# An attention and MLP kernel on one core: an earlier front with fp32 beacon transposes, and batch 1's k and q loaded ahead of the last quarter of the first weight matrix

## The chip, the cores and the metric

One core of one Trainium2 chip. The metric is the device time of one execution in microseconds (us). Quoted times are medians of fast executions; most executions of one kernel lie within 1 us of its median, single ones up to 4 us above it. An execution more than 1.5% above the fastest of its kernel is called slow here and left out of every ratio. The span that a trace shows is about 1.7 us shorter than the time.

## The reference

Attention for 8 batches of 8 heads over 576 tokens, with 16 "beacon" keys and values ahead of each sequence, then an MLP with a squared relu over all 4608 tokens. In short:

```python
# q, k, v: [8, 8, 576, 64]; beacon_k, beacon_v: [8, 8, 16, 64]
# w_in: [512, 2048]; w_out: [2048, 512]
k_all = np.concatenate([beacon_k, k], axis=2)
v_all = np.concatenate([beacon_v, v], axis=2)
scores = np.matmul(q, k_all.transpose(0, 1, 3, 2)) / np.sqrt(64)
scores = np.where(causal, -1e9, scores)
a = softmax(scores)
x = np.matmul(a, v_all).transpose(0, 2, 1, 3).reshape(4608, 512)
g = np.maximum(x @ w_in, 0.0) ** 2
out = g @ w_out
```

## The kernel before

The program is a list of operations with modelled durations. A scheduler of the kernel's own, run while the program is built, sorts them into one fixed order for each engine; on the chip each engine runs its list in that order and waits by semaphores only for data and buffers. Where the model sees TensorE idle in the first 22 us it inserts a filler, a product of zeros, meant to have the array at full clock early.

```python
    def emit_fill(bank, cols):
        nc.tensor.matmul(ps[bank][:, 0:cols], g[1][:, 0, 0:128], g[1][:, 0, 0:cols], start=True, stop=True)
...
    # Order.run: nothing is ready for engine e at the modelled time now
    if e == "PE" and 0.3 < now < self.FILL_UNTIL and self.pools["ps"]:
        cols = 128 if now < 7.0 else 256
        ...
```

Transfers of the first two batches and of the weights go through GpSimd's queue one behind the other (`t` tables, `p1k` pair 1's k, `v0` the first part of v, `w0` a quarter of w_in); then comes batch 1's k and q, then batch 1's v.

```python
    SOFT = "t0 p1k p1q t1 p2k p2q v0 v1 p3k p3q v2 v3 v4 w0 w1 w2 w3".split()
    ...
    strided[1, 0, 0, "k"].behind[:] = chain[-1:]
    v_loads[1][0].behind[:] = [strided[1, 0, HP - 1, "q"]]
```

A v part lands as fp32 and GpSimd casts it to bf16. VectorE applies the causal masks, does relus together with ScalarE, and squares. TensorE's first layer writes into one of four PSUM banks, which comes free when the relu has read it.

```python
        def emit_cast(e):                      # GpSimd, for batch 1's v
            st = stg[ld.held[2]]
            if x == "v":
                copy_on(e, vb[b % 2][0:rows, c, :, 0:D], st[0:rows])
        ...
        def emit_mask(e):                      # VectorE, two inputs in SBUF
            ...
                nc.vector.tensor_tensor(out=d, in0=d, in1=tri[:, m0:m0 + m, :][:, None].to_broadcast([128, 2, m, 128]),
                                        op=ALU.min)
        ...
        def emit_relu(e, ft=ft, lo=lo_ - t0, hi=hi_ - t0, box=box):
            h = ps[box["s1"].held[2]][:, 0:hi - lo]       # one input, in PSUM
            ...
                nc.vector.tensor_scalar(out=dst, in0=h, scalar1=0.0, scalar2=None, op0=ALU.max)
        ...
        def emit_sq(e, f=f, lo=lo_ - t0, hi=hi_ - t0):    # two inputs in SBUF
            nc.vector.tensor_tensor(out=d, in0=d, in1=d, op=ALU.mult)
```

The softmax here doesn't subtract the row's maximum and nothing guards it: scores larger than these inputs give would overflow.

Of the kernel before, what the change touches and what calls it, by code (L numbers as in the profile page):

```python
# [9 lines left out]
FP32 = mybir.dt.float32  # L10
# [36 lines left out]
class Order:  # L47
# [22 lines left out]
    def run(self):  # L70
# [16 lines left out]
        free = {e: 2.3 if e == "DVE" else 0.0 for e in engines}  # L87
        dma_free = 0.0
        lanes = {"SP": [], "POOL": [], "ACT": []}
        events = [(0.0, 0, None, None)]  # L90
# [3 lines left out]
        now = 0.0  # L94
        while events:
# [19 lines left out]
            while again:  # L115
                again = False
                for e in engines:
# [26 lines left out]
                    if best is None:  # L144
                        if e == "PE" and 0.3 < now < self.FILL_UNTIL and self.pools["ps"]:
                            cols = 128 if now < 7.0 else 256
                            free[e] = now + 0.107
                            issued.append((Op("fill", "PE", 0.107, lambda e, cols=cols, bank=self.pools["ps"][0]: self.fill(bank, cols)), e, now))
                            seq += 1
                            heapq.heappush(events, (free[e], seq, "free", None))  # L150
                        continue
# [51 lines left out]
def kernel(  # L203
# [63 lines left out]
    bkf = [sb("bkf", [Nb, H, D], FP32)] * 2  # L267
    bks = [sb(f"bks{i}", [Nb, H, D], BF16) for i in range(2)]
# [45 lines left out]
    ident_op = add("ident", "POOL", 1.3, lambda e: make_identity(nc, ident), prio=-300.0)  # L314
    tri_ops = [add(f"tri{i}", "POOL", (0.95, 0.55)[i], lambda e, i=i: emit_tri(e, i), prio=-250.0) for i in range(2)]
# [39 lines left out]
    def add_load(b, x, c, prio, behind=[], sync=[]):  # L355
# [34 lines left out]
        if x != "v":  # L390
            if b < NPE + 2:
                deps += [zero_ops[b]]
            else:
# [4 lines left out]
                            late=(5.0 if b else 1) if x == "v" else 0.0)  # L398

    def add_trans(b, x, prio):  # L400
        srcb, dst = (qb, qT) if x == "q" else (kb, kT)

        def emit(e):
            nc.sync.dma_start(
                out=dst[b % 2].rearrange("p g (c t) -> p (g c) t", c=NT),
                in_=srcb[b % 2].rearrange("p g c d -> p (g c d)"),
                transpose=True,
            )

        deps = [cast[b, x, c] for c in range(NT)]  # L410
        deps += [o for p in range(HP * (b - 2), HP * (b - 1)) for o in qk_ops[p]]
        trans[b, x] = [add(f"tr{b}{x}", "SP", 4.1, emit, prio=prio, deps=deps, dma=3.7, late=3.0)]

    def add_beacon(b, prio):
        prio = prio if b else -299.5
        ld = add(f"bkl{b}", "SP", 0.45, lambda e: [nc.sync.dma_start(
            out=bkf[b % 2], in_=beacon_k[b].transpose([1, 0, 2]))], prio=prio, dma=0.1,
                 deps=[cast[b - 1, "bk"]] if b else [])
        bk = add(f"bkc{b}", "DVE", 0.4, lambda e: nc.vector.tensor_copy(bks[b % 2], bkf[b % 2]), prio=prio,
                 deps=[ld])  # L420
        cast[b, "bk"] = bk
        if b:
            bk.need.extend(norm_ops[HP - 1, 0])
        box = {}

        def emit_tp(e):
            pp = ps[box["t"].held[2]].bitcast(BF16)
            for pr in range(HP):
                nc.tensor.transpose(pp[:, pr * Nb:(pr + 1) * Nb], bks[b % 2][:, 2 * pr:2 * pr + 2, :], ident[0:Nb, 0:Nb])

        busy = [o for pr in range(HP) for o in qk_ops[HP * (b - 2) + pr]] if b >= 2 else []
        box["t"] = add(f"tpb{b}", "PE", 0.25, emit_tp, prio=prio - 100.0, deps=[bk, ident_op], take=("ps", "tp"))

        def emit_ev(e):
            pp = ps[box["t"].held[2]].bitcast(BF16)
            copy_on(e, kT[b % 2][:, :, 0:Nb], pp[:, 0:HP * Nb].rearrange("p (g n) -> p g n", g=HP))

        bk_ev[b] = add(f"ekb{b}", "DVE", 0.2, emit_ev, prio=-200.0, deps=[box["t"]] + busy, give=box["t"])

    bk_ev = {}  # L440

# [17 lines left out]
    def add_strided(b, prio):  # L459
# [7 lines left out]
        for part, (t0, np_, ns, prs) in enumerate(parts_of[b]):  # L467
            n_tok = np_ * ns
            own = b == 0 and part < 2
            for pr in prs:  # L470
                groups = ["kq"] if 2 * n_tok <= 1024 else ["k", "q"]
                for n, xs in enumerate(groups):
# [20 lines left out]
                    for i, x in enumerate(xs):  # L493
# [6 lines left out]
                        if b == 0:  # L500
                            engs = ("DVE",)
                        else:
                            engs = ("DVE",) if x == "k" else ("DVE", "ACT")
                        ev = add(f"e{x}{b}.{part}.{pr}", engs,
                                 {"DVE": 0.12 + n_tok / 960.0, "ACT": 0.2 + n_tok / 1200.0}, emit_ev,
                                 prio=(-200.0 if x == "k" else -199.0) + 0.01 * part, deps=[tp])
# [5 lines left out]
    def add_first_loads():  # L512
        first = []
        at = 0
        for part in range(2):
            t0, np_, ns, _ = parts_of[0][part]
            for n, (x, t) in enumerate((("k", k), ("q", q))):
# [3 lines left out]
                def emit(e, t=t, n=n, raw=raw, t0=t0, np_=np_, ns=ns):  # L521
# [3 lines left out]
                o = add(f"fld{x}{part}", ("SP", "ACT")[n], (0.45, 0.55)[n], emit, prio=-300.0 + part,  # L525
                        dma={"k": (0.3, 0.75), "q": (0.55, 0.65)}[x][part])
                first.append(o)

                def emit_cast(e, x=x, raw=raw, part=part):
                    copy_on(e, paired_buf(x, part).rearrange("p s (u d) -> p u s d", u=2), raw)  # L530

                strided[0, part, 0, x] = add(f"fc{x}{part}", ("DVE", "ACT")[n],
                                             ((0.33, 0.75)[part], (0.42, 0.52)[part])[n], emit_cast,
                                             prio=-210.0 + part, deps=[o], late=0.3)
# [63 lines left out]
    RANK = [(0, 0), (0, 1), (1, 0), (2, 0), (1, 1), (3, 0), (2, 1), (3, 1)]  # L598
# [37 lines left out]
    PLAN = ((2,2,3,3,3),(2,2,3,3,3),(2,3,3,3,2),(2,3,3,3,2),(2,3,3,3,2),(2,3,3,3,2),(2,3,3,3,2))  # L636
# [339 lines left out]
    SOFT = "t0 p1k p1q t1 p2k p2q v0 v1 p3k p3q v2 v3 v4 w0 w1 w2 w3".split()  # L976
# [60 lines left out]
    v_loads[1][0].behind[:] = [strided[1, 0, HP - 1, "q"]]  # L1037
# [33 lines left out]
```

## Time and profile before

| before | |
|---|---|
| time, median of 4 runs | 337.98 us (337.48 to 338.21) |
| span of the trace | 335.8 us |
| TensorE busy | 327.9 us, 98% |
| TensorE's waits for another engine | 1.1 us at the start, 0.7 us for batch 1's first k |
| full clock from | 4.2 us |

TensorE sets the time. How the lines are read is told with the prediction, which shows the front and the wait. These are VectorE, GpSimd and TensorE in the timeline of the kernel before (start, length, engine, line, operation, shapes, count, idle before with its releaser):

```profile
41.70 0.94 DVE L712 TENSOR_TENSOR pt<-pt,tri 128x512 bf16<-128x512 bf16 x2
...
39.29 0.62 POOL L327 CAST vb<-stg 128x512 bf16<-128x512 f32 x1 [0.22 <-DMA stg<-in_v_dram]
40.78 0.70 POOL L327 CAST vb<-stg 80x512 bf16<-80x512 f32 x1
...
41.61 2.38 PE L901 MATMUL ps<-xT,w_in 128*128 128x272 bf16 x20
```

Two masks take 0.94 us together. They begin at 41.70, 0.22 us after GpSimd's last cast of batch 1's v has ended (41.48); the matmuls of the first layer have no wait.

### The profile page before, as it was taken

How to read it: one execution, taken by the hardware profiler on the slowest of the kernel's cores; microseconds unless marked ns; L12 is line 12 of the kernel's file. 1: busy time of each engine (PE TensorE's matmuls, PEld its weight loads, DVE VectorE, ACT ScalarE, POOL GpSimd, SP SyncE). 2: the span in 40 equal slices, each digit the busy share in tenths (PEclk: the TensorE clock that was granted, in tenths of full speed). 3: DMA queues.
4: the chain of work that ended last, by engine and by line, in shares of the span. 5: the costliest groups of instructions: out<-in, count | busy, mean ns of one | idle time of the engine just before them, and what ended most of it. 6: DMA issues, size and time to landing. Idle time of an engine off the chain costs nothing.

```text
span 335.8 us, 7815 instructions
## 1 busy us (share of the span) xinstructions
PE 327.9 (98%) x3156; PEld 188.1 (56%) x3197; DVE 170.8 (51%) x389; ACT 191.1 (57%) x291; POOL 92.7 (28%) x145
## 2 busy tenths in 40 slices
PE   8999999999999999999999999999999999999996
PEld 7586765544654655555459845554555544444444
DVE  5786885238645983477147733573457302301400
ACT  4976865377638827565466655666457216515621
POOL 9874803316404614041134132423000000000000
PEclk9999999999999999999999999999999999999999
DMA  8999989999999999899799997999210221011003
GB/s 153 193 207 220 208 143 208 222 240 211 193 215 232 197 184 184 185 232 176 146 239 235 174 186 183 249 186 167 76 62 2 46 90 62 0 64 62 1 2 124
DMA packets 143955, 51.74 MB, mean 154 GB/s; under 512 B 130702, under 2 KB 138798, under 8 KB 143918
## 3 DMA queue, kind: packets, MB, share of 16 engines
q1 hardware_dynamic: 135375, 42.19, 61.6%
q0 software_dynamic: 7904, 8.69, 14.9%
q8 instruction: 25, 0.41, 0.5%
q10 hardware_dynamic: 639, 0.36, 0.4%
q14 instruction: 12, 0.10, 0.1%
HBM read 37.22 MB, written 9.44 MB: 139 GB/s over the span
## 4 chain that ended last, share of the span: by engine, by line
PE 89%; DMA 5%; POOL 4%; issue 1%; ACT 0%; POOLq 0%
PE ps L901 36%; PE ps L939 36%; PE ps L738 8%; PE strip L620 5%; DMA qk_area<-in_k_dram 3%; PE ps L620 2%; DMA stg<-in_v_dram 2%; POOL qk_area L449 1%; PE ps L851 1%; PE ps L484 1%; POOL stg L371 1%; PE ps L805 1%; POOL w_in L830 0%; POOL vb L327 0%; POOL tri L311 0%
## 5 line engine op out<-in xcount | busy, mean ns | idle before, releaser
L901 PE MATMUL ps<-xT,w_in 128*128 128x512 bf16 (+3 forms) x689 | 133.3, 340 | 0.9 <-issue 0.2
L939 PE MATMUL ps<-w_out,g 128*128 128x512 bf16 x534 | 126.3, 379 | 2.0 <-issue 0.8
L901 PEld LDWEIGHTS <-w_in 128*128 128x128 bf16 x704 | 65.4, 98 | 51.4 <-issue 0.7
L917 ACT ACTIVATE g<-ps 128x512 bf16<-128x512 f32 (+2 forms) x118 | 66.3, 562 | 43.1 <-PE ps L901 42.5
L629 ACT ACTIVATE pt<-strip 128x1024 bf16<-128x1024 f32 (+3 forms) x86 | 81.3, 1002 | 12.1 <-PE strip L620 11.9
L926 DVE TENSOR_TENSOR g<-g 128x1024 bf16<-128x1024 bf16 (+2 forms) x80 | 52.7, 666 | 63.3 <-ACT g L917 62.2
L939 PEld LDWEIGHTS <-g 128*128 128x128 bf16 x560 | 51.5, 98 | 56.8 <-issue 1.7
L327 POOL CAST qk_area<-stg 128x512 bf16<-128x512 f32 (+2 forms) x60 | 40.3, 677 | 61.5 <-DMA stg<-in_k_dram 35.1
L325 ACT COPY osb<-ps 128x512 f32<-128x512 f32 (+2 forms) x29 | 16.4, 569 | 65.2 <-PE ps L939 60.5
L327 POOL CAST vb<-stg 128x512 bf16<-128x512 f32 (+1 forms) x40 | 26.4, 671 | 70.7 <-DMA stg<-in_v_dram 67.3
L738 PEld LDWEIGHTS <-pt 128*128 128x128 bf16 (+1 forms) x960 | 36.2, 97 | 10.1 <-DVE pt L712 0.2
L738 PE MATMUL ps<-vb,pt 128*128 128x65 bf16 (+1 forms) x960 | 39.0, 194 | 0.0
L712 DVE TENSOR_TENSOR pt<-pt,tri 128x512 bf16<-128x512 bf16 x64 | 29.6, 472 | 12.0 <-ACT pt L629 6.7
L757 DVE TENSOR_TENSOR xn<-ps,rcp 128x320 bf16<-128x320 f32 (+2 forms) x64 | 31.5, 492 | 2.3
L919 DVE TENSOR_SCALAR g<-ps 128x512 bf16<-128x512 f32 (+2 forms) x42 | 24.7, 606 | 13.8 <-PE ps L901 13.2
L671 ACT ACTIVATE pt<-ps 128x512 bf16<-128x512 f32 x42 | 22.8, 597 | 13.7 <-PE ps L620 11.1
L620 PEld LDWEIGHTS <-kT 64*128 64x128 bf16 x596 | 19.8, 94 | 16.0 <-issue 14.2
L755 DVE RECIPROCAL rcp<-ps 128x5 f32<-128x5 f32 (+2 forms) x64 | 12.2, 191 | 30.0 <-PE ps L738 29.1
L620 PE MATMUL strip<-qT,kT 64*128 64x208 bf16 (+13 forms) x474 | 27.0, 239 | 0.0
L327 DVE COPY osb<-ps 128x512 f32<-128x512 f32 (+1 forms) x9 | 5.8, 647 | 33.4 <-PE ps L939 17.4
L295 PE MATMUL ps<-g 128*128 128x128 bf16 (+1 forms) x83 | 10.1, 274 | 1.1 <-DVE warm L302 1.1
L371 POOL DMA_DIRECT2D stg<-in_v_dram x10 | 8.5, 859 | 5.7 <-DMA w_in<-in_moe_w_in_dram 4.4
(42 smaller groups left out, 98.3 us busy)
## 6 DMA issues: line engine op xcount, KB each, us to landing
out_dram<-osb SPq DMA_DIRECT2D x17, 512.0 KB, 4.1
stg<-in_q_dram SPq DMA_DIRECT2D x24, 256.0 KB, 5.1
stg<-in_k_dram SPq DMA_DIRECT2D x18, 256.0 KB, 5.1
stg<-in_v_dram SPq DMA_DIRECT2D x18, 256.0 KB, 4.5
w_in<-in_moe_w_in_dram POOLq DMA_DIRECT2D x4, 512.0 KB, 8.1
w_out<-in_moe_w_out_dram POOLq DMA_DIRECT2D x4, 512.0 KB, 11.1
stg<-in_v_dram POOLq DMA_DIRECT2D x6, 256.0 KB, 7.6
stg<-in_k_dram SPq DMA_DIRECT2D x6, 224.0 KB, 4.5
```

The source lines that it names most:

```text
L327: eng[e].tensor_copy(dst, src)
L620: nc.tensor.matmul(st[hj][:, at:at + t1 - t0], kT[b % 2][hp, pr, 128 * c:128 * c + 128], qT[b % 2][hp, pr, t0:t1], start=True, stop=True,)
L629: nc.scalar.activation(pt[:, :, at:at + width], strips[qk.slots[s]][:, :, 0:width], AF.Exp, bias=0.0, scale=scale)
L671: nc.scalar.activation(pt[:, hj, at:at + 512], ps[qk.wide[hj]], AF.Exp, bias=0.0, scale=scale)
L712: nc.vector.tensor_tensor(out=d, in0=d, in1=tri[:, m0:m0 + m, :][:, None].to_broadcast([128, 2, m, 128]), op=ALU.min)
L738: nc.tensor.matmul(a[:, at + (t - tl[0]) * (D + 1):at + (t - tl[0] + 1) * (D + 1)], P[0:rr, hj, o:o + 128], vb[b % 2][0:rr, c, 2 * pr + hj ...
L757: nc.vector.tensor_tensor(out=xn[b % 2].rearrange("p t (h d) -> p h t d", d=D)[:, h0:h0 + nh, tl[0]:tl[0] + nt], in0=a[:, :, :, 0:D], in1= ...
L901: nc.tensor.matmul(h[:, lo - spans[0][0]:hi - spans[0][0]], w_in_sb[:, mc, ft * 128:(ft + 1) * 128], xT[:, mc, lo % RING:lo % RING + hi - lo],
L917: nc.scalar.activation(dst, h, AF.Relu, bias=0.0, scale=1.0)
L919: nc.vector.tensor_scalar(out=dst, in0=h, scalar1=0.0, scalar2=None, op0=ALU.max)
L926: nc.vector.tensor_tensor(out=d, in0=d, in1=d, op=ALU.mult)
L939: nc.tensor.matmul(o, G[:, fc, ts * 128:(ts + 1) * 128], w_out_sb[:, fc, :], start=(fc == 0), stop=(fc == NFT - 1))
```

## The change

The intent: begin real work sooner (k cast and transposed without waiting for q, the beacon transposed in fp32 without a cast), load the last pair's q and k ahead of v, and take away TensorE's wait for batch 1's k by loading batch 1's k and q ahead of w_in's last quarter. The core of the diff:

```diff
-                        if e == "PE" and 0.3 < now < self.FILL_UNTIL and self.pools["ps"]:
-                            cols = 128 if now < 7.0 else 256
+                        if e == "PE" and 0.9 < now < self.FILL_UNTIL and self.pools["ps"]:
+                            cols = 128 if now < 6.0 else 256
...
+    ident32_op = add("ident32", "DVE", 0.1, lambda e: nc.vector.tensor_copy(ident32, ident[0:Nb, 0:Nb]), prio=-300.0, deps=[ident_op])
...
-                            late=(5.0 if b else 1) if x == "v" else 0.0)
+                            late=(5.0 if b > 2 else 3.0 if b else 1) if x == "v" else 0.0)
...
-        bk = add(f"bkc{b}", "DVE", 0.4, lambda e: nc.vector.tensor_copy(bks[b % 2], bkf[b % 2]), prio=prio,
-                 deps=[ld])
...
-                nc.tensor.transpose(pp[:, pr * Nb:(pr + 1) * Nb], bks[b % 2][:, 2 * pr:2 * pr + 2, :], ident[0:Nb, 0:Nb])
+                nc.tensor.transpose(ps[box["t"].held[2]][:, pr * Nb:(pr + 1) * Nb], bkf[:, 2 * pr:2 * pr + 2, :], ident32)
...
-                groups = ["kq"] if 2 * n_tok <= 1024 else ["k", "q"]
+                groups = ["kq"] if 2 * n_tok <= 1024 and not own else ["k", "q"]
...
-    PLAN = ((2,2,3,3,3),(2,2,3,3,3),(2,3,3,3,2),(2,3,3,3,2),(2,3,3,3,2),(2,3,3,3,2),(2,3,3,3,2))
+    PLAN = ((2,2,3,3,3),(2,2,2,2,2,2,1),(2,3,3,3,2),(2,3,3,3,2),(2,3,3,3,2),(2,3,3,3,2),(2,3,3,3,2))
...
-    SOFT = "t0 p1k p1q t1 p2k p2q v0 v1 p3k p3q v2 v3 v4 w0 w1 w2 w3".split()
+    SOFT = "t0 p1k p1q t1 p2k p2q p3k p3q v0 v1 v2 v3 v4 w0 w1 w2".split()
...
-    v_loads[1][0].behind[:] = [strided[1, 0, HP - 1, "q"]]
+    w_ops["in", 3].behind[:] = [strided[1, 0, HP - 1, "q"]]
+    v_loads[1][0].behind[:] = [w_ops["in", 3]]
```

Left out: modelled durations of the first loads and casts, a choice of engines for them, a rank of score phases, and names.

More of the change, by code (lines that the diff above doesn't have):

```diff
@@ L86, in run @@
                 release(op)
-        free = {e: 2.3 if e == "DVE" else 0.0 for e in engines}
+        free = {e: {"DVE": 2.3, "ACT": 0.05}.get(e, 0.0) for e in engines}
         dma_free = 0.0
         lanes = {"SP": [], "POOL": [], "ACT": []}
-        events = [(0.0, 0, None, None)]
+        events = [(0.0, 0, None, None), (0.05, 0, None, None)]
         seq = 0
@@ L265, in paired_buf @@
             "p (s e) -> p s e", s=parts_of[0][part][2])
-    bkf = [sb("bkf", [Nb, H, D], FP32)] * 2
-    bks = [sb(f"bks{i}", [Nb, H, D], BF16) for i in range(2)]
+    bkf = sb("bkf", [Nb, H, D], FP32)
+    ident32 = sb("ident32", [Nb, Nb], FP32)
     vb = [sb(f"vb{i}", [128, NT, H, D + 1], BF16) for i in range(2)]
@@ L411, in add_trans @@
         deps += [o for p in range(HP * (b - 2), HP * (b - 1)) for o in qk_ops[p]]
-        trans[b, x] = [add(f"tr{b}{x}", "SP", 4.1, emit, prio=prio, deps=deps, dma=3.7, late=3.0)]
+        trans[b, x] = [add(f"tr{b}{x}", "SP", 4.1, emit, prio=prio, deps=deps, dma=3.7, late=3.0 if b > 2 else 1.5)]
     def add_beacon(b, prio):
-        prio = prio if b else -299.5
+        prio = prio if b else -298.5
         ld = add(f"bkl{b}", "SP", 0.45, lambda e: [nc.sync.dma_start(
-            out=bkf[b % 2], in_=beacon_k[b].transpose([1, 0, 2]))], prio=prio, dma=0.1,
-                 deps=[cast[b - 1, "bk"]] if b else [])
-        bk = add(f"bkc{b}", "DVE", 0.4, lambda e: nc.vector.tensor_copy(bks[b % 2], bkf[b % 2]), prio=prio,
-                 deps=[ld])
-        cast[b, "bk"] = bk
-        if b:
-            bk.need.extend(norm_ops[HP - 1, 0])
+            out=bkf, in_=beacon_k[b].transpose([1, 0, 2]))], prio=prio, dma=0.1,
+                 deps=[bk_tp[b - 1]] if b else [])
         box = {}
         def emit_tp(e):
-            pp = ps[box["t"].held[2]].bitcast(BF16)
             for pr in range(HP):
-                nc.tensor.transpose(pp[:, pr * Nb:(pr + 1) * Nb], bks[b % 2][:, 2 * pr:2 * pr + 2, :], ident[0:Nb, 0:Nb])
+                nc.tensor.transpose(ps[box["t"].held[2]][:, pr * Nb:(pr + 1) * Nb], bkf[:, 2 * pr:2 * pr + 2, :], ident32)
         busy = [o for pr in range(HP) for o in qk_ops[HP * (b - 2) + pr]] if b >= 2 else []
-        box["t"] = add(f"tpb{b}", "PE", 0.25, emit_tp, prio=prio - 100.0, deps=[bk, ident_op], take=("ps", "tp"))
+        box["t"] = bk_tp[b] = add(f"tpb{b}", "PE", 0.25, emit_tp, prio=prio - 100.0,
+                                  deps=[ld, ident32_op] + (norm_ops[HP - 1, 0] if b else []), take=("ps", "tp"))
         def emit_ev(e):
-            pp = ps[box["t"].held[2]].bitcast(BF16)
-            copy_on(e, kT[b % 2][:, :, 0:Nb], pp[:, 0:HP * Nb].rearrange("p (g n) -> p g n", g=HP))
+            copy_on(e, kT[b % 2][:, :, 0:Nb], ps[box["t"].held[2]][:, 0:HP * Nb].rearrange("p (g n) -> p g n", g=HP))
         bk_ev[b] = add(f"ekb{b}", "DVE", 0.2, emit_ev, prio=-200.0, deps=[box["t"]] + busy, give=box["t"])
     bk_ev = {}
+    bk_tp = {}
     def add_part_load(b, part, prs, x, prio, behind, free, dma, late=0.0):
@@ L500, in add_strided @@
                         if b == 0:
-                            engs = ("DVE",)
+                            engs = ("ACT", "DVE") if own and part == 1 and x == "q" else ("DVE",)
                         else:
@@ L505, in add_strided @@
                                  {"DVE": 0.12 + n_tok / 960.0, "ACT": 0.2 + n_tok / 1200.0}, emit_ev,
-                                 prio=(-200.0 if x == "k" else -199.0) + 0.01 * part, deps=[tp])
+                                 prio=(-200.0 if x == "k" else -199.0) + 0.01 * part - (500.0 if b == 0 and part == 2 else 0.0), deps=[tp])
                         evs.append(ev)
@@ L523, in emit @@
                         out=raw, in_=t[0, 0:2, t0:t0 + np_ * ns, :].rearrange("h (p s) d -> p h s d", s=ns))]
-                o = add(f"fld{x}{part}", ("SP", "ACT")[n], (0.45, 0.55)[n], emit, prio=-300.0 + part,
-                        dma={"k": (0.3, 0.75), "q": (0.55, 0.65)}[x][part])
+                o = add(f"fld{x}{part}", ("SP", "ACT")[n], (0.6, 0.55)[n], emit, prio=-300.0 + part,
+                        dma={"k": (0.43, 0.15), "q": (0.37, 0.85)}[x][part])
                 first.append(o)
@@ L530, in emit_cast @@
                     copy_on(e, paired_buf(x, part).rearrange("p s (u d) -> p u s d", u=2), raw)
-                strided[0, part, 0, x] = add(f"fc{x}{part}", ("DVE", "ACT")[n],
-                                             ((0.33, 0.75)[part], (0.42, 0.52)[part])[n], emit_cast,
-                                             prio=-210.0 + part, deps=[o], late=0.3)
+                strided[0, part, 0, x] = add(f"fc{x}{part}", (("DVE",), ("ACT",))[n] if part == 0 or x == "q" else ("ACT", "DVE"),
+                                             {"DVE": (0.46, 0.6)[part], "ACT": (0.42, 0.52)[part]}, emit_cast,
+                                             prio=-210.0 + 20.0 * part, deps=[o], late=0.1)
             at += 2 * ns * D
@@ L597 @@
     NSPLIT = HP
-    RANK = [(0, 0), (0, 1), (1, 0), (2, 0), (1, 1), (3, 0), (2, 1), (3, 1)]
+    RANK = [(0, 0), (0, 1), (1, 0), (1, 1), (2, 0), (3, 0), (2, 1), (3, 1)]
     def phases(p):
```

## The prediction

> **What bounds the kernel now.** I read the page first, then TensorE's list of waits, then its timeline over the first 38 us, then the chain of waits and the landings of the transfers in the same stretch.
>
> The page and TensorE's list of waits, the whole kernel:
>
> ```profile
> PE 327.9 (98%) x3156; PEld 188.1 (56%) x3197; DVE 170.8 (51%) x389; ACT 191.1 (57%) x291; POOL 92.7 (28%) x145
> L295 PE MATMUL ps<-g 128*128 128x128 bf16 (+1 forms) x83 | 10.1, 274 | 1.1 <-DVE warm L302 1.1
> ...
> PE ps L295 <- DVE warm L302: 1.1, 1, 1.1
> PE ps L939 <- issue: 0.8, 5, 0.2
> PE ps L484 <- DMA qk_area<-in_k_dram: 0.7, 1, 0.7
> PE ps L901 <- issue: 0.2, 1, 0.2
> ```
>
> TensorE works 327.9 of 335.8 us. It waits for another engine just twice: 1.1 us at the start, and 0.7 us for batch 1's first k. The 0.2 us entries marked "issue" have the length of one 512-column matmul (216 ns from start to start) and lie between equal matmuls, many of them about 10.8 us apart: records missing from the trace, not waits. But 83 of TensorE's matmuls are fillers (L295, zeros into a spare bank), put into its fixed order wherever the kernel's own scheduler thought it would be idle. They always run. So "98% busy" holds some 8 us of nothing, and the time is the sum of a fixed list plus its waits.
>
> TensorE's timeline where the change bites:
>
> ```profile
> 1.12 3.40 PE L295 MATMUL ps<-g 128*128 128x128 bf16 x32 [1.12 <-DVE warm L302]
> 4.37 0.38 PE L481 MATMUL ps<-ident,qk_area 120*128 120x120 bf16 x4
> 4.68 0.25 PE L429 MATMUL ps<-ident,bks 16*128 16x16 bf16 x4
> 4.86 1.01 PE L295 MATMUL ps<-g 128*128 128x128 bf16 x15
> 5.80 0.47 PE L481 MATMUL ps<-ident,qk_area 112*128 112x112 bf16 x6
> 6.20 0.34 PE L620 MATMUL strip<-qT,kT 64*128 64x240 bf16 x4
> ...
> 10.25 0.83 PE L295 MATMUL ps<-g 128*128 128x256 bf16 x6
> 11.01 0.35 PE L620 MATMUL strip<-qT,kT 64*128 64x336 bf16 x4
> ...
> 24.49 1.39 PE L901 MATMUL ps<-xT,w_in 128*128 128x240 bf16 x12
> 25.72 0.31 PE L805 MATMUL ps<-ident,xn 128*128 128x128 bf16 x3
> 25.87 2.78 PE L901 MATMUL ps<-xT,w_in 128*128 128x240 bf16 x24
> 29.37 0.70 PE L484 MATMUL ps<-ident,qk_area 96*64 96x96 bf16 x24 [0.71 <-DMA qk_area<-in_k_dram]
> ```
>
> Columns: start, length, engine, line, tiles, count, idle before. Between 1.12 and 28.6 us TensorE never idles: in the front it arrives later than its operands, because of the fillers. At 29.37 it is early.
>
> The chain of waits over the same stretch names the loads behind that wait:
>
> ```profile
> 16.07 1.36 POOL vb L327 x2
> 17.43 1.42 POOL w_in L830 x2
> 18.84 10.48 DMA qk_area<-in_k_dram
> 29.32 0.04 issue
> 29.37 0.70 PE ps L484 x24
> ```
>
> The load takes 10.48 us because it stands in the GpSimd queue behind w_in. From the landings: w_in's quarters at 22.8, 25.3 and 28.0 us (the last issued at 18.1, 9.9 to land), then batch 1's k and q at 29.3, 30.8, 32.3 and 33.8. So a quarter costs 2.7 us of that queue, a half batch of k or q 1.5.
>
> [...]fillers of 128 columns start 107 ns apart until 4.3 us, then 56 ns. [...]six 256-column fillers, 109 ns apart, take 0.65 us, and the scores after them start 0.76 us after the first; I count about 0.09 us at each switch. [...]the first k load (120 KB) takes 2.6 us to land, so there is nothing to gain ahead of 3.4 us.[...]
>
> **The change, part by part**, read from the order in which both programs' instructions stand on each engine. I take the TensorE list from the first transpose up to batch 1's first k transposes: in the kernel before that is 4.37 to about 28.49 us, 24.12 us of work.
>
> Start. The fillers ahead of the first transpose go from 32 to 21, so they end at 1.12 + 21 x 0.107 = 3.37. k alone then needs its load (0.80 + 2.6 = 3.4) and the 0.46 us cast on VectorE: about 3.95. So TensorE starts real work at 4.0 instead of 4.37: -0.37, with 0.6 us of idle time in place of fillers. q's own cast (3.85 + 0.40) is ready for its turn.
>
> First scores. k part 1 is loaded ahead of the beacon: issued at about 1.3 instead of 1.74, so landed at 4.7. VectorE casts it to 5.3, then still has q's copy and the beacon's copy before the scores. Those start at about 6.0 against 6.20: the VectorE beacon cast (0.49 us at 4.13) is gone, but much of it is given to other work in the same order.
>
> Fillers in the stretch: of 128 columns 18 become 12, of 256 columns 33 become 40: -6 x 0.056 + 7 x 0.109 = +0.43.
>
> Beacon transposes. Four bf16 ones (0.18 us between starts) become four fp32 ones, each loading its own weights.[...] Mode switches stay at 40.
>
> First-layer work. Because batch 1's k comes sooner, the order puts fewer first-layer matmuls ahead of it: of 240 columns 24 instead of 36, of 272 columns 4 instead of 12: -12 x 0.1025 - 8 x 0.117 = -2.17. This is moved, not saved.
>
> So the stretch lasts 24.12 + 0.43 + 0.6 - 2.17 = 22.98, and TensorE reaches batch 1's k at 4.0 + 22.98 = 26.98. With w_in's last quarter behind it, that k lands at 29.3 - 2.7 = 26.6, perhaps a little sooner, as the v loads no longer wait for a cast. The wait vanishes; the other three land at 28.1, 29.6 and 31.1, each ahead of its turn.
>
> Compared at equal work: 26.98 + 2.17 = 29.15 against 29.37, a gain of 0.22 us. The saving is the wait removed plus the earlier start[...]. After this the list is the same work in another order: batch 2's scores in seven groups instead of five add two switches over the whole kernel, 0.19 us. Sum: -0.03, call it nothing. I lean a little lower, -0.3, because the fp32 guess may be high and because I can see no wait that the removed one could become: w_in's last quarter now lands at about 33.8, its first use by my count of the list is near 40 us.
>
> The last pair's q and k ahead of v lands them at about 10.2 and 11 us instead of 13.1 and 14.0; v's first two parts slip by 0.8 and 1.5 us to about 12.5 and 13.9. The first products with v stand at about 16.5, so neither is on the path. Part 1's q copy on ScalarE takes 0.45 us ahead of the first exponential; the second still doesn't wait for more than TensorE's order. The exponentials should end somewhat sooner than 21.9, but TensorE's fixed list hides that.
>
> **Rivals.** First: the exponentials set the front. ScalarE runs almost without a break from 7.94 to 17 us, and ends at 21.93; if TensorE's fillers only filled holes that ScalarE made, an earlier start would carry through and the front would shorten by 0.8 to 1.5 us: 336.5 to 337.2. For it: the change looks made for this. Against: ScalarE's waits in the front are for TensorE (3.3 us in six waits for scores), and TensorE waits for nothing.
>
> Second: the clock opens[...]. The idle 0.6 us before 4.0, and single fillers between waits, could leave the array at half clock[...]: +1 to +1.5 us, 338.7 to 339.2. For it: [...]the list before has no idle time in it. Against: three quarters of it are still busy.
>
> Third: fp32 transposes cost 1 us or more each time[...]: +1 to +1.5, some 338.5 to 339. Nothing in the trace speaks for or against.
>
> Fourth: VectorE is late. Its work for the norms in 17 to 25 us is tight (4.54 of 5 us busy between 15 and 20), and it now casts a part of v (0.6 us): a few waits of 0.1 to 0.3 us on TensorE, in all up to +0.5.
>
> **Range and chances.** The centre is 337.99 - 0.3 = 337.7. Downwards the first rival gives some 0.8 to 1; upwards the second, third or fourth about 1.2; run-to-run spread is 0.4 either way. So 336.8 to 339.0. A change of 2% would be 6.8 us: more than half of everything that the front's fillers and waits hold, on a program whose later 306 us stay the same work. Faster 0.015, within 2% 0.975, slower 0.01.
>
> **What would show it.** Right: TensorE's wait for batch 1's k gone or under 0.2 us, its first transpose at about 4.0, batch 1's k transposes near 27.0[...], and busy time after 30 us the same within 0.5. Wrong in the first rival's way: batch 1's transposes at 26.4 or sooner. In the second's: 128-column fillers still 107 ns apart after 5 us. In the third's: a group of fp32 transposes over 1 us. The prediction falls altogether if a new wait of over 1 us shows on TensorE between 30 and 50 us, on w_in's last quarter, batch 1's v or w_out.

The sum came to 24.12 + 0.43 + 0.6 - 2.17 = 22.98 us for the stretch, 26.98 us for batch 1's k and -0.03 for the kernel; its +0.6, a guess for the fp32 transposes, rests on no trace. Without that term the sums are 22.38, 26.38 and -0.63. The second rival is that the array stays at half clock longer; its +1 to +1.5 us rested on a length of half clock that no trace had shown.

## The result, and the profile after

The changed kernel takes 340.44 us (339.93 to 340.64, 4 runs) against 337.98 (337.48 to 338.21, 4 runs) for the kernel before: ratio 1.0072, interval 1.0055 to 1.0090. A ratio is the mean time of one kernel's fast runs over that of the other's in the same rounds, so it is not quite the ratio of the medians. The change costs about 2.5 us where a gain of 0.3 was predicted, and the time lies outside the predicted range.

The page and TensorE's list of waits of the changed kernel:

```profile
PE 333.5 (98%) x3187; PEld 188.5 (56%) x3187; DVE 168.4 (50%) x387; ACT 191.7 (57%) x290; POOL 92.7 (27%) x144
...
PE ps L477 <- DVE qk_area L328: 0.4, 1, 0.4
PE ps L801 <- DVE xn L753: 0.4, 1, 0.4
PE ps L424 <- DMA bkf<-in_beacon_k_dram: 0.2, 1, 0.2
```

The wait for batch 1's k is gone. The waits at the start of real work (0.4 and 0.2) and one at 101.9 us for a norm (0.4) do not add up to the loss. TensorE's busy time grew by 5.6 us, but this trace has all its 3187 matmuls and the other lacks 41 of its 3197 (the weight loads, PEld, are complete), so the growth is not evidence by itself. The timeline shows where the time is:

```profile
1.12 2.42 PE L295 MATMUL ps<-g 128*128 128x128 bf16 x21 [1.12 <-DVE warm L302]
3.97 0.38 PE L477 MATMUL ps<-ident,qk_area 120*128 120x120 bf16 x2 [0.42 <-DVE qk_area L328]
4.14 0.42 PE L295 MATMUL ps<-g 128*128 128x128 bf16 x2
...
5.46 0.60 PE L424 MATMUL ps<-ident,bkf 16*128 16x16 f32 x4 [0.15 <-DMA bkf<-in_beacon_k_dram]
6.00 0.82 PE L295 MATMUL ps<-g 128*128 128x128 bf16 x6
...
7.73 1.25 PE L295 MATMUL ps<-g 128*128 128x256 bf16 x5
...
24.30 0.42 PE L424 MATMUL ps<-ident,bkf 16*128 16x16 f32 x4
...
29.84 0.70 PE L480 MATMUL ps<-ident,qk_area 96*64 96x96 bf16 x24
```

At 7.73 us five 256-column fillers take 1.25 us; six of them took 0.83 us in the kernel before. From start to start they are 213 ns apart, against 109: the array is at half clock. By the starts of single matmuls it stays there until about 11.15 us (transposes of 96 columns start 79 ns apart up to 10.3 us and 42 from 11.18 on), while in the kernel before full clock came at 4.2. So batch 1's transposes (29.84) begin 0.47 us later than before, although there are 2.16 us less first-layer work ahead of them. The figure for the granted clock is no help: it is 1.0 for this execution and 0.999 for the one before, and 0.999 or 1.0 in every other profiled one, e4's slow one included.

I counted the stretch from the first transpose to batch 1's first k transposes from single matmuls: columns at full clock, 0.093 us for each change of tiling mode (the rows and columns that stand in a line as 128*128 or 64*128; in the kernel before, the last 256-column filler of a run, at 8.74, 10.80 or 11.52 us, is followed by the next transpose or score after 202 to 205 ns instead of 109), and the rest as excess.

| us | before | after | predicted step | measured step |
|---|---|---|---|---|
| first transpose at | 4.37 | 3.97 | -0.37 | -0.40 |
| fillers | 4.61 | 5.04 | +0.43 | +0.43 |
| beacon transposes | 0.20 | 0.50 | +0.60 | +0.30 |
| first-layer work | 5.08 | 2.92 | -2.17 | -2.16 |
| excess: waits and half clock | 1.74 | 4.06 | -0.71 | +2.32 |
| batch 1's k transposes at | 29.37 | 29.84 | -2.4 | +0.47 |

The rest of the stretch is equal within 0.02. (The predicted steps add up to -2.2; the prediction has 26.98, that is -2.4, as it took the end of the work ahead of the wait 0.17 us too early.) Only one step differs much, and it is the second rival of the prediction: of the 4.06 us some 3.1 are half clock.

### The profile page after: what moved, and what is told of

Same layout as the page of the kernel before. It is cut to its first block, busy times and chain, and to the rows that moved or that the text cites. A ratio compares the mean times of both kernels' runs of the same rounds, so it can differ in the third digit from the quotient of the medians.

```text
span 338.8 us, 7819 instructions
## 1 busy us (share of the span) xinstructions
PE 333.5 (98%) x3187; PEld 188.5 (56%) x3187; DVE 168.4 (50%) x387; ACT 191.7 (57%) x290; POOL 92.7 (27%) x144
## 3 DMA queue, kind: packets, MB, share of 16 engines
q1 hardware_dynamic: 135375, 42.19, 62.2%
## 4 chain that ended last, share of the span: by engine, by line
PE 97%; DMA 1%; DVE 1%; ACT 0%; issue 0%; SPq 0%; DVEq 0%
PE ps L897 37%; PE ps L935 36%; PE ps L734 9%; PE strip L616 7%; PE ps L295 2%; PE ps L616 2%; PE ps L480 2%; PE ps L801 1%; DMA bkf<-in_beacon_k_dram 1%; PE ps L847 1%; DVE xn L753 0%; PE ps L424 0%; SPq L518 0%; ACT xT L326 0%; DVE rcp L751 0%
## 5 line engine op out<-in xcount | busy, mean ns | idle before, releaser
L897 PE MATMUL ps<-xT,w_in 128*128 128x512 bf16 (+3 forms) x704 | 134.8, 340 | 0.0
L935 PE MATMUL ps<-w_out,g 128*128 128x512 bf16 x560 | 130.6, 379 | 0.0
L913 ACT ACTIVATE g<-ps 128x512 bf16<-128x512 f32 (+2 forms) x123 | 69.2, 562 | 50.0 <-PE ps L897 48.0
L625 ACT ACTIVATE pt<-strip 128x1024 bf16<-128x1024 f32 (+3 forms) x89 | 84.5, 1003 | 21.2 <-PE strip L616 20.8
L326 ACT COPY osb<-ps 128x512 f32<-128x512 f32 (+2 forms) x26 | 14.6, 566 | 49.1 <-PE ps L935 45.7
L616 PE MATMUL strip<-qT,kT 64*128 64x112 bf16 (+14 forms) x490 | 28.5, 242 | 0.0
L915 DVE TENSOR_SCALAR g<-ps 128x512 bf16<-128x512 f32 (+2 forms) x37 | 21.8, 600 | 9.3 <-PE ps L897 9.0
L667 ACT ACTIVATE pt<-ps 128x512 bf16<-128x512 f32 x36 | 19.5, 598 | 11.5 <-PE ps L616 10.2
L328 DVE COPY osb<-ps 128x512 f32<-128x512 f32 (+1 forms) x12 | 7.9, 658 | 35.4 <-PE ps L935 23.6
L295 PE MATMUL ps<-g 128*128 128x256 bf16 (+1 forms) x73 | 11.5, 305 | 1.1 <-DVE warm L302 1.1
## 6 DMA issues: line engine op xcount, KB each, us to landing
w_out<-in_moe_w_out_dram POOLq DMA_DIRECT2D x4, 512.0 KB, 10.9
```

The costliest lines, as they stand in the source:

```text
L328: eng[e].tensor_copy(dst, src)
L616: nc.tensor.matmul(st[hj][:, at:at + t1 - t0], kT[b % 2][hp, pr, 128 * c:128 * c + 128], qT[b % 2][hp, pr, t0:t1], start=True, stop=True,)
L625: nc.scalar.activation(pt[:, :, at:at + width], strips[qk.slots[s]][:, :, 0:width], AF.Exp, bias=0.0, scale=scale)
L667: nc.scalar.activation(pt[:, hj, at:at + 512], ps[qk.wide[hj]], AF.Exp, bias=0.0, scale=scale)
L897: nc.tensor.matmul(h[:, lo - spans[0][0]:hi - spans[0][0]], w_in_sb[:, mc, ft * 128:(ft + 1) * 128], xT[:, mc, lo % RING:lo % RING + hi - lo],
L913: nc.scalar.activation(dst, h, AF.Relu, bias=0.0, scale=1.0)
```

## The experiments

The theory after the first trace (A): the thinner fillers, with holes at 3.5 and 5.3 us, let the clock open late. A rival (B): the load order does the harm, through a wait that this first trace does not show. Both had to be separated, since the change holds both. (In the expectations of the first two calls A is called CLOCK; LOADS and FP32 say that the load order or the fp32 transposes cost the time.)

Eighteen kernels ran, in five calls; a call shares its runs of the kernel before, whose median was 337.78, 338.11, 337.68, 338.18 and 338.01. All results are correct except e13's.

### First call: the head and the loads

**e1**: the changed kernel with six more fillers ahead of the first k transposes. The edit, in the loop that emits the planned list, is also the one that later "dense" kernels extend:

```diff
             if e != "-":
+                if op.name == "tp0.0.0k":
+                    for _ in range(6):
+                        self.fill(0, 128)
                 op.insts = op.emit(e)
```

> The changed kernel with 6 more 128-column fillers ahead of the first k transpose (27 instead of 21), nothing else moved. Theory CLOCK (the 0.6 us hole at 3.4 us keeps the array at half clock until 10.7 us): fillers fall to 56 ns apart before 5 us, batch 1's first k transposes start at 27.0 to 27.6 us instead of 29.84, and the time falls by 2.0 to 2.8 us to about 337.6 to 338.4. Theory FP32 (the fp32 beacon transposes cost the time) or LOADS (the new order of loads does): six fillers of 107 ns fill idle time only, so 340.2 to 340.6, as the changed kernel.

339.44 us (338.80 to 340.01), ratio 1.0044 (1.0026 to 1.0063). The hole at 3.5 us was filled, a wait of 0.41 us for the beacon at 5.76 stayed, and the clock opened at 9.7 us. So one filled hole is not enough; about 1 us is gained over the ratio of the changed kernel, less than A expected and more than its rivals did.

**e2**: the kernel before with 11 of its first 32 fillers dropped.

```diff
+        skip = 11
         for op, e, _ in issued:
+            if op.name == "fill" and skip:
+                skip -= 1
+                continue
```

> The kernel before with its first 32 fillers cut to 21, nothing else moved. CLOCK: an idle stretch of about 1 us ahead of the first transpose at 4.35 us keeps fillers 107 ns apart beyond 5 us, perhaps to 8 or 11; the kernel before has 0.9 us of slack ahead of batch 1's k, so the time rises by 0.7 to 2.2 us to 338.7 to 340.2. FP32 and LOADS: neither is touched, the time stays at 338.0 within 0.3.

338.43 us, ratio 1.0044 (1.0006 to 1.0081), with two of six executions at 341.3 and 341.7. In the profiled one half clock lasted until 8.1 us instead of 4.2, so fewer fillers went with a later clock there; but batch 1's k transposes came at 29.76 instead of 29.37, since the wait for the load was used up. The median lies between what the theories expected. With the old loads a late clock is mostly absorbed.

**e3**: the changed kernel with the bf16 beacon copy put back.

```diff
-                nc.tensor.transpose(ps[box["t"].held[2]][:, pr * Nb:(pr + 1) * Nb], bkf[:, 2 * pr:2 * pr + 2, :], ident32)
+                nc.tensor.transpose(ps[box["t"].held[2]].bitcast(BF16)[:, pr * Nb:(pr + 1) * Nb], bks[b % 2][:, 2 * pr:2 * pr + 2, :], ident[0:Nb, 0:Nb])
```

(The cast on VectorE and its tile return with it.)

> The changed kernel with the beacon cast to bf16 on VectorE and transposed in bf16 again, as before; the hole ahead of the first k transpose stays. CLOCK: half clock still until about 8 to 11 us, time 339.8 to 340.8[...]. FP32: back to 338.0 within 0.5. LOADS: as the changed kernel, 340.4.

340.98 us, ratio 1.0088 (1.0067 to 1.0109): no better. The fp32 transposes are not the cause. In its trace the clock opened at 7.7 us, and a wait of 1.2 us for a relu on VectorE appeared near 41 us: the first sign of B.

**e4**: the changed kernel with the loads in the old order.

```diff
-    SOFT = "t0 p1k p1q t1 p2k p2q p3k p3q v0 v1 v2 v3 v4 w0 w1 w2".split()
+    SOFT = "t0 p1k p1q t1 p2k p2q v0 v1 p3k p3q v2 v3 v4 w0 w1 w2 w3".split()
...
-    w_ops["in", 3].behind[:] = [strided[1, 0, HP - 1, "q"]]
-    v_loads[1][0].behind[:] = [w_ops["in", 3]]
+    v_loads[1][0].behind[:] = [strided[1, 0, HP - 1, "q"]]
```

> The changed kernel with the order of loads of before (v's first two parts ahead of the last pair's q and k; all of w_in ahead of batch 1's q and k). CLOCK: half clock still until 8 to 11 us; batch 1's first k then lands near 29.3 us, which at half clock is no wait, so 340.0 to 341.0. LOADS: back to 338.0 within 0.5. FP32: as the changed kernel.

337.93 us in three fast runs, ratio 1.0000 (0.9977 to 1.0022), and one slow run of 343.47, the profiled one, in which half clock lasted until 19.0 us. That is what LOADS expected; A had expected 340 to 341, a miss. Everything else in the change is free as long as the loads stay. This says that the load order is needed for the loss, not how it makes it.

### Second call: both causes apart

**e5**: the changed kernel with a dense head: fillers `{"tp0.0.0k": 6, "tp0.0.0q": 2, "tpb0": 6}` in the loop of e1, 14 in all.

> The changed kernel with 14 more 128-column fillers: 6 ahead of the first k transpose, 2 ahead of the first q transpose, 6 ahead of the beacon's, so that TensorE has no hole from 1.1 to about 6 us. CLOCK[...]: full clock between 4 and 7 us in the trace, batch 1's first k transposes at 27.0 to 28.4 us, and a time of 337.6 to 338.8, 1.6 to 2.8 us below the changed kernel, with no run above 340. If the loads[...] cost the time: 340.2 to 341, since 14 fillers are only added.

339.53 us, ratio 1.0044 (1.0028 to 1.0060). Its profiled execution (338.64, its lowest) does what the prediction said of the front: clock at 4.6 us, batch 1's k transposes at 27.41, which is 26.97 without the 0.44 us of extra fillers (26.98 was predicted; that it agrees so closely is luck, since errors of the prediction offset each other: fp32 transposes 0.30 us too high, the end of the work 0.17 too early). And yet it is no faster than the kernel before, and a miss for A, which expected 337.6 to 338.8 and no run above 340 (one took 340.26): TensorE then waits 0.7 us for a relu at about 41 us, and 0.4 us for a norm.

**e6**: e5 with the second entry of `PLAN` and both `late` values of the kernel before.

> As e5_dense_head, with the plan of batch 2's scores and the slack for later casts and transposes as in the kernel before. CLOCK sees nothing in it. If TensorE's new 0.4 us wait for a norm at 102 us comes from the new plan, that wait goes and the time is 0.2 to 0.6 us below e5_dense_head; if not, the same within 0.3 and the wait stays.

339.99 us, ratio 1.0055: a miss; the plan is not to blame. The wait for the relu was 1.4 us, and waits for norms took 1.4 us in three places instead of 0.4 in one.

**e7**: the changed kernel, unedited, as control.

> The changed kernel once more, unedited, for a second trace and more times. CLOCK: full clock at some other moment between 7 and 18 us than 10.7, the time moving with it by about half of the difference, and never as early as 5 us; most runs 339.5 to 341. If the half clock is not what varies: 340.4 within 0.4 in all runs whatever the trace shows.

340.41 us, ratio 1.0082 (1.0044 to 1.0120), one run at 344.42. Its profiled execution was its lowest (339.43): the clock opened at 4.6 us, which A had ruled out for this head ("never as early as 5 us"), and TensorE waited 1.33 us for a relu at 42.19. So the changed kernel itself has the wait of B, and a late clock hides it.

**e8**: the kernel before with the new load order alone (the reverse of e4's edit).

> The kernel before with only the new order of loads (last pair's q and k ahead of v, batch 1's q and k ahead of the last quarter of w_in); its 32 first fillers stay, so full clock near 4.3 us. The order puts 16 240-column and 12 272-column first-layer matmuls less ahead of batch 1's k, so TensorE is there at about 25.7 us and the load at 26.6: CLOCK expects a wait of 0.5 to 1 us and 337.8 to 338.6, as before within 0.5. If the loads are what costs the time in the changed kernel: 339.5 or more. If they are a gain that the clock hid: 337.2 or less.

339.87 us, ratio 1.0045 (1.0029 to 1.0062), with the head of 32 fillers and the clock at 4.2 us. A wait of 0.94 us for a relu on VectorE at 42.87 us, and one of 0.8 for a norm. A had expected 337.8 to 338.6, a miss. So B needs neither the new head nor a late clock.

What precedes that wait is best seen in the changed kernel with an early clock (e18, clock at about 5 us): the timeline of VectorE, GpSimd and TensorE.

```profile
39.35 1.57 DVE L708 TENSOR_TENSOR pt<-pt,tri 128x512 bf16<-128x512 bf16 x2
40.85 0.64 DVE L712 TENSOR_TENSOR pt<-pt,tri 80x160 bf16<-80x160 bf16 x1
41.41 1.75 DVE L915 TENSOR_SCALAR g<-ps 128x272 bf16<-128x272 f32 x5
...
39.54 0.51 POOL L352 MEMSET qk_area<- 128x512 bf16 x1
40.01 1.38 POOL L328 CAST vb<-stg 128x512 bf16<-128x512 f32 x2
...
41.89 2.78 PE L897 MATMUL ps<-xT,w_in 128*128 128x272 bf16 x24 [1.19 <-DVE g L915]
```

The two masks take 1.57 us instead of 0.94, the small one 0.64 instead of 0.23, in the stretch in which GpSimd casts. (The first took 824 ns although most of it lies beside a memset and the next cast is recorded only 0.66 us after its start; so the recorded starts do not show which of GpSimd's instructions goes with a slow mask.) Five relus stand behind them in VectorE's order, and TensorE, whose four banks are full, waits 1.19 us for the first. In the kernel before TensorE reached that place behind more first-layer work, and the masks came after the casts.

Other work of VectorE points to the casts as well. In e7 three squares of 544 columns, which like the masks have two inputs in SBUF, took 1.99 us from 37.74 on, beside casts from 37.25 to 39.42, where one at 46.36, with GpSimd idle, took 0.44. The relu of 272 columns at 37.39 has one input, in PSUM; it ran beside those casts too and took 0.43 us, as one in the kernel before at 44.35 did with GpSimd idle. That had still to be tested, as VectorE's order alone could make the wait.

### Third call: the casts moved to ScalarE

**e9**: e5 with the casts of batch 1's last two v parts on ScalarE. **e11**: the same in e8.

```diff
-        engs = ("POOL", "DVE") if b == 0 and c <= 1 else ("POOL",)
+        engs = ("POOL", "DVE") if b == 0 and c <= 1 else ("ACT",) if b == 1 and x == "v" and c >= 3 else ("POOL",)
```

> e5 (the changed kernel with the dense head) with the casts of batch 1's last two v parts on ScalarE instead of GpSimd. Theory B (the time is given back at 41 to 43 us, where VectorE's masks run 0.7 to 0.9 us instead of 0.41 us beside GpSimd's casts and TensorE waits 0.7 to 1.4 us for the relus behind them): the masks there take 0.40 to 0.45 us, TensorE's wait for a relu there is under 0.3 us, and the time is 0.5 to 1.0 us below e5's 339.5, so 338.5 to 339.0. Rival (the two engines do not disturb each other; the wait comes from the order of VectorE's work alone): the masks stay at 0.7 us or more or the wait of 0.7 us or more stays though they are short, and the time is 339.2 or more.

338.81 us, ratio 1.0026 (1.0007 to 1.0044): the time falls as expected and the masks take 420 and 424 ns, but a wait of 0.99 us for a relu stands at 40.20. It is another one: the cast on ScalarE waits 2.27 us for its load, and relus stand behind it in ScalarE's order. So the edit confounds the test.

> e8 (the kernel before with the new load order alone) with batch 1's last two v casts on ScalarE. Theory B: the wait of 0.94 us for a relu at 42.87 us falls under 0.3 us, and the time falls from e8's 339.9 by 0.5 to 1.0 us, to 338.9 to 339.4; what is left over before's 338.0 is the wait of 0.8 us for a norm and the lost overlap. Rival (the contention is beside the point): 339.6 or more, with the wait in place.

338.79 us, ratio 1.0026 (1.0005 to 1.0047); masks of 420 and 426 ns, the wait 0.28 us. As expected (the time even 0.1 us lower), but the scheduler had shifted relus between engines too.

**e10**: e4 with the dense head of e5. **e12**: e4 again.

> e4 (the changed kernel with the loads in the order of before) plus the 14 fillers of e5. Theory A (the thin filler runs at 3.4 and 5.1 us let the clock open late in many executions) says that with e4's loads this gains little on the median, since the wait for batch 1's k absorbs a late clock, but takes away the slow executions of 343 us: 337.3 to 338.1, no run above 340, clock open before 7 us in the trace. Rival (only the loads mattered, the clock not): the same median as e4, 337.9, but again with some run of 341 us or more in six. If the extra fillers only cost their time: 338.5.

338.14 us, ratio 1.0002 (0.9981 to 1.0022), no slow run in six, the clock at 7.1 us: as expected, just outside the expected time, and no better than the kernel before.

> e4 over again, unedited, for a trace in the usual state (e4's own profiled execution was its slow one). Both theories: 337.6 to 338.1. Theory B says that in this trace TensorE waits 0.3 to 1 us for batch 1's k at 27 to 30 us as before, and has no wait over 0.4 us between 36 and 50 us. Rival: a wait of 0.7 us or more for a relu is there as in e5 to e8, and something else makes up for it.

338.31 us, ratio 1.0014 (0.9989 to 1.0039), 0.2 us above the range expected. No wait at all between 36 and 50 us, as theory B said. The other half missed: there was no wait for batch 1's k, because the clock opened only at 9.5 us in this execution and TensorE came at 31.01.

### Fourth call: the same order, without the reading

**e13**: e5 with GpSimd's last two v casts replaced by memsets of the same tiles. Nothing moves in any engine's order; GpSimd just reads no SBUF there.

```diff
+            if b == 1 and x == "v" and c >= 3:
+                nc.gpsimd.memset(vb[b % 2][0:rows, c, :, 0:D], 0.0)
-            if x == "v":
+            elif x == "v":
                 copy_on(e, vb[b % 2][0:rows, c, :, 0:D], st[0:rows])
```

> Wrong result on purpose: e5 with GpSimd's casts of batch 1's v parts 3 and 4 replaced by GpSimd memsets of the same tiles, so that GpSimd does as many instructions at the same places in every engine's order but reads no SBUF there. Theory B[...]: the masks at 39 to 41 us take 0.40 to 0.45 us each instead of e5's 0.88 and 0.71, TensorE's wait for the relus is under 0.2 us, and the time is 0.5 to 0.9 us below e16's. Rival (order alone): the wait stays at 0.5 us or more and the time within 0.3 us of e16's.

**e16**, its control, is e5 unedited.

> e5 over again, unedited, as the control for e13 and e14 on the same chip: ratio to before 1.003 to 1.006 and a wait of 0.5 us or more for a relu at 40 to 43 us under theory B. Under the rival that e5's wait was an accident of one execution there is none.

e16 took 339.56 us (338.99 to 340.34), e13 338.64 (338.37 to 339.23): 0.92 us less, just over the most that was expected. The timelines, e16 first:

```profile
40.56 1.62 DVE L710 TENSOR_TENSOR pt<-pt,tri 128x512 bf16<-128x512 bf16 x2
...
40.54 1.37 POOL L330 CAST vb<-stg 128x512 bf16<-128x512 f32 x2
...
42.73 2.47 PE L899 MATMUL ps<-xT,w_in 128*128 128x272 bf16 x21 [1.53 <-DVE g L917]
```

and e13:

```profile
40.33 0.87 DVE L712 TENSOR_TENSOR pt<-pt,tri 128x512 bf16<-128x512 bf16 x2
...
40.67 0.98 POOL L385 MEMSET vb<- 128x512 bf16 x2
...
39.73 4.80 PE L901 MATMUL ps<-xT,w_in 128*128 128x272 bf16 x40
```

In both, GpSimd works beside the masks. Where it casts, they take 1.62 us and TensorE waits 1.53; where it only writes, 0.87 us, and 40 matmuls run without a break. So the casts are the cause of the wait, and order alone is refuted. Whether it is their reading of SBUF or their longer time (1.37 us for the two casts, 0.98 for the two memsets of the same tiles) e13 does not tell apart.

**e14**: e5 with the two casts planned behind the mask that they met; GpSimd clears its next two tiles first. **e15**: the same in e8.

```diff
+    named = {o.name: o for o in order.ops}
+    for c in (3, 4):
+        named[f"cast1v{c}"].need.append(named["mask4.0"])
```

> e5 with batch 1's last two v casts planned after the mask that they met (GpSimd clears its next two tiles first). Correct result. Theory B: as e13, masks of 0.40 to 0.45 us, wait under 0.3 us, 0.5 to 0.9 us below e16. Rival: within 0.3 us of e16, or the casts meet the squares instead and the wait only moves.

338.27 us (338.02 to 338.49), 1.29 us below e16 and more than expected; ratio to the kernel before 0.9996 (0.9958 to 1.0034). The two masks take 413 and 426 ns, the small one still meets a cast (645 ns), and the wait is 0.23 us. Part of the gain is not the contention: the edit shifted the order later on too, and the wait of 0.4 us for a norm near 101 us, which e13 and e16 have, is gone. With these costs out of the way the change costs nothing, and gains nothing that these runs can tell from the kernel before. The interval is wide as the kernel before had runs of 339.99 and 341.63.

> e8 (the kernel before with the new load order alone) with the same two casts planned after the mask. Theory B: e8's wait of 0.94 us at 42.87 us is under 0.3 us, and the ratio to before is 1.0015 to 1.003 instead of e8's 1.0045. Rival: 1.004 or more.

339.00 us (337.78 to 340.89), ratio 1.0018 (0.9974 to 1.0062). Inside the expected ratio, but the spread leaves it inconclusive: the second mask (716 ns) still met a cast, and waits of 0.3 to 0.5 us took the place of the one of 0.94.

### Fifth call: the casts planned later, alone

**e17**: e14's edit in the changed kernel, without extra fillers. **e18**: the changed kernel, unedited, as its control.

> The changed kernel with only the two v casts planned after the mask, no extra fillers. If the late clock and the contention at 40 to 43 us are two separate costs of which the first hides the second in some executions: ratio to before 1.003 to 1.006, so 0.5 to 1.2 us below e18 and 0.6 to 1.5 us above what e14 had against before (0.9996); in the trace no wait over 0.3 us for a relu at 39 to 44 us, whenever the clock opens. Rival (the contention was the whole of the loss and the fillers of e14 do nothing): ratio as e14's, 0.999 to 1.001. Rival (the clock was the whole): as e18.

> The changed kernel unedited, control for e17 on the same chip: ratio to before 1.006 to 1.009. Its trace has either half clock until 8 us or later and no relu wait of 0.7 us at 40 to 43 us (as its first trace), or an early clock and that wait (as e7).

e17 340.24 us, ratio 1.0049 (1.0019 to 1.0079); e18 340.24, ratio 1.0061 (1.0033 to 1.0088). The expectation of 0.5 to 1.2 us failed: the medians are equal. One execution of e17 took 338.15, the other five 340.04 to 340.42. The trace of a usual one shows why the cure didn't hold (VectorE, GpSimd, TensorE):

```profile
40.61 2.14 DVE L708 TENSOR_TENSOR pt<-pt,tri 128x512 bf16<-128x512 bf16 x2
...
40.86 1.16 POOL L328 CAST vb<-stg 128x512 bf16<-128x512 f32 x2
...
43.31 1.91 PE L897 MATMUL ps<-xT,w_in 128*128 128x272 bf16 x16 [0.89 <-DVE g L915]
```

Here the clock opened late, at 9.0 us, so TensorE and with it the mask came 0.9 us later than in e14, into the very casts that were planned behind it. The first mask is recorded as starting 0.25 us before the first cast, yet ran 1.68 us where the second took about 0.4, past both casts, which took 0.60 and 0.61 us. The plan gives GpSimd an order, not a wait: nothing on the chip holds the cast back for the mask.

## Why the prediction was wrong, point by point

**The start.** Right, with some luck: 3.97 us for the first transpose, where 4.0 was predicted. k landed at 3.58 instead of 3.4, and its cast took 0.31 us instead of 0.46. The first scores did not follow: 7.31 us instead of 6.0, at half clock (6.10 in e7 and 6.34 in e18, whose clock opened early).

**Fillers, first-layer work, switches.** Right: +0.43 and -2.16, as worked out. Over the whole kernel there are 123 changes of tiling mode instead of 121.

**Beacon transposes.** Right in kind, half the guess: 0.30 us in both groups together, not 0.6. At full clock a group of four took 0.42 us in fp32 (the changed kernel, 24.30 us) and 0.25 in bf16 (the kernel before, 4.68), with starts 62 and 25 ns apart; the trace shows one matmul for each. e3 shows that taking the fp32 out again gains nothing.

**The loads.** Right: batch 1's first k landed at about 26.7 us (predicted 26.6), w_in's last quarter at about 34 (predicted 33.8), and TensorE's wait for k was gone. The last pair's k and q landed at 10.9 and 11.7 (predicted 10.2 and 11), v's first two parts at 13.2 and 14.1 (12.5 and 13.9), and no wait came of it.

**The clock: the first failed step.** The sum set "0.6 us of idle time in place of fillers" down as a gain of 0.37 us, and the second rival was put aside with "three quarters of it are still busy". In the changed kernel's first trace half clock until 11.15 us cost some 3.1 us, in the way that this rival named, and about twice what it named. The kernels with the dense head (e5, e6, e9, e10, e13, e14, e16) had the clock open between 4.2 and 7.1 us in all seven traces, those with the 32 fillers of before (the kernel before, e8, e11, e15) between 4.2 and 6.3; those with a thin head (the changed kernel's first look, e1, e2, e3, e4, e12, e17) between 7.7 and 19.0 in seven of nine, and at 4.6 and about 5 in e7 and e18. So it varies between executions of one kernel, and density shifts the odds. The dense head is worth 0.9 us of the median (e5 against e7). That a late clock also explains the usual execution of the changed kernel is an inference: its profiled executions with the early clock took 339.43 and 339.07, the others of the same calls 340.02 to 341.07 without the one of 344.42, but only profiled executions show their clock.

17 of the 20 packed traces (array 0/clock of trace.npz) hold the moment at which the full clock began: 11.16 us in the first trace of the changed kernel, 4.19 in the kernel before. Beside the waits in the front they show no rule. In the first trace of the changed kernel TensorE waited 0.42 us for its first transpose and 0.15 for the beacon; e18, with the same list, waited 0.18 and 0.17 and had full clock at about 5 us; e4 waited 0.42 for its first transpose and got it at 19.0; e3 waited 0.77 and got it at 7.7; e10 waited for nothing after the start and got it at 7.1. So "three quarters of it are still busy" was no safe argument, and theory A, by which full clock needs a stretch with hardly a hole, was too strict. What decides between the two states of one kernel is not shown.

**"I can see no wait that the removed one could become": the second failed step.** With an early clock there is one, of 1.2 to 1.3 us at 42 us (e7, e18), in the stretch and of the size at which the prediction said that it would fall. It is not a wait for w_in's last quarter, for batch 1's v or for w_out, as it named them, but for a relu, which is late because batch 1's v is being cast. With the wait for k gone and less first-layer work ahead, TensorE and VectorE come there 2.4 us sooner in e18 (first mask at 39.35 instead of 41.70), while the last two v parts land nearly as before (39.03 and 39.55 us against 39.24 and 39.67), so VectorE's masks fell on GpSimd's casts of them. e8 shows it without the new head, e13 that the casts make it.

**How the two share the loss.** The four combinations, as ratios to the kernel before:

| | thin head | dense head |
|---|---|---|
| new loads | 1.0072, 1.0082, 1.0061 | 1.0044 (e5), 1.0035 (e16) |
| new loads, casts planned later | 1.0049 (e17) | 0.9996 (e14) |
| old loads | 1.0000 (e4), 1.0014 (e12) | 1.0002 (e10) |

The 1.0082 includes the run of 344.42, which falls just short of slow; without it the ratio is 1.0062. The costs don't add. Planning the casts later without the fillers (e17) leaves the median where it was, but in its trace the casts met the masks all the same, so the contention was not cured there; curing the clock alone gains 0.9 us, both together about 2 (338.27 against the 340.24 to 340.44 of the changed kernel in other calls; some 0.4 of it is the norm's wait). A late clock hides the contention of one order (masks of 0.87 us and no such wait in the changed kernel's first trace) and moves the other order into it (2.14 and a wait of 0.89 in e17); the old loads absorb a late clock in the wait for k, and keep the masks off the casts.

For the first trace itself the difference of 3.0 us in span adds up from single matmuls, with the gaps of missing records taken out: up to 50 us the excess (waits and half clock) is about 6.3 us against 3.9, +2.4; the norm at 101.9 us +0.40; fp32 transposes +0.30; two switches +0.19; fillers over the whole kernel 6.21 against 6.39, -0.18. The sum is +3.1.

**The norms.** The fourth rival was right in size: 0.18 us of excess near 20 us, and 0.4 at 101.9, later than it was expected.

**What stays open.** What decides when the full clock begins; what in a cast slows a mask; a clock record for the executions that were not profiled; and e15, which can't be told from no effect. No version beats both kernels: e4, e10 and e14 are within their intervals of the kernel before.

## What to carry to other kernels

Removing a wait of a full engine moves everything behind it against work that runs on transfer time (here the first mask by 2.4 us, the last v parts by 0.2 or less), so look through the next 20 us for what the moved work will stand beside before counting the wait as gained: two masks on VectorE took 1.62 us beside GpSimd's casts (e16) and 0.87 beside its memsets (e13). A filler ahead of the first real matmul is not idle time to be saved: in the changed kernel's first trace, with holes of 0.42 and 0.15 us ahead of real work, half clock until 11.16 us cost some 3.1 us; in e18, with holes of 0.18 and 0.17, full clock came at about 5 us, and one trace does not tell how often each comes. A plan that only orders an engine's work does not keep two engines apart (in e17 the masks ran into the casts planned behind them and took 2.14 us); check a cure at an early and at a late clock.
